# Weight bounds from products of the weight tiles with themselves, and scales kept for four groups of tiles

## The chip, the cores and the metric

The kernel runs on one core of a Trainium2 chip. Its five engines work side by side, each through its own queue in order: TensorE (PE, with its weight loads as PEld), VectorE (DVE), ScalarE (ACT), GpSimd (POOL), and SyncE (SP), which issues the DMAs. The metric is the device time of one execution in microseconds (us); the kernel before takes 956.86 us, the median of 3 runs between 954.78 and 958.99.

## What is computed

Clustered attention is followed by a two-layer network. A query sees only the keys that fall to the same of 16 centroids. The two weight matrices come as 64-bit floats, the other inputs as 32-bit ones; batch 4, 8 heads, 768 positions, head width 64, model width 512, hidden width 2048 (`attn_out` below is `attn` times `v`).

```python
q_assign = np.argmax(np.einsum('bhsd,hcd->bhsc', q_n, c_n), axis=-1)
k_assign = np.argmax(np.einsum('bhsd,hcd->bhsc', k_n, c_n), axis=-1)
mask = q_assign[:, :, :, None] == k_assign[:, :, None, :]
scores = scale * np.matmul(q, k.transpose(0, 1, 3, 2))
scores = np.where(mask, scores, -1000000000.0)
scores = scores - np.max(scores, axis=-1, keepdims=True)
attn = np.exp(scores)
attn = attn / (np.sum(attn, axis=-1, keepdims=True) + 1e-09)
...
x = np.ascontiguousarray(attn_out.transpose(0, 2, 1, 3)).reshape(B * S, H * D)
h = x @ w_in
r = np.maximum(h, 0.0)
g = s * (r * r) + b
return (g @ w_out).astype(np.float32)
```

## The kernel before, in words

Every product is made from float16 pairs, a high and a low part, in three matmuls, so each operand is first scaled by a power of two that a bound on its size gives.

**Units.** The attention is cut into 192 units (one batch, one head, 128 queries). The main loop runs once for each: unit i has its scores on PE (L454, tile `sc`), its maximum on DVE (L463), its exponential on ACT (L473, tile `p`), and one turn later the high part `ph` (L483, `high`), the low part on POOL (L496), and a transposing DMA (L498); the product with the values (L515 to L517, tile `px`) comes five turns later. The first eight units (`RAW`) go through PE transposes instead. `high` casts on POOL for units 8 to 18, then up to unit 36 in turn on DVE (odd) and ACT (even), then on ACT.

**MLP steps.** With a lag of 21 turns (`LAG`), turn i also runs step i-21 of the MLP: 12 matmuls into `h` (L573), three ACT passes (L580 to L583), a POOL subtraction (L588), and two turns later 6 matmuls into `acc` (L600). There are 12 chunks of 16 steps; step ft uses the weight tiles ft of both matrices. `acc`, `h` and `px` have one PSUM buffer each; small helpers use the banks of `h` and `px`.

**Weights.** 32 tiles (16 of each matrix, numbered p, w_in even and w_out odd) go through `weights()`: a load of 512 KB, `rebase` (ACT, L203), `narrow` (two DVE instructions, L207 and L208), and one stage later `bound`: an ACT pass with absolute values (L215 or L217), for w_in also four matmuls with ones (L220) and a DVE reduction (L221). Three stages run ahead of the loop and each turn runs two more, so the last tile is done around turn 15. `finish_w_in` and `finish_w_out` then make one scale for each matrix with a row of tiny DVE instructions into `glob`. `wsplit(ft)` (from turn 17 on, one each turn, ACT L265 and DVE L267) makes the float16 pairs of step ft. At the end of the first chunk `column_sums` (L275, 32 matmuls into `pb`) makes the `bias` row, and two DVE instructions (L608) write out `acc`.

A scheduler orders each engine's queue: code order is the priority, units up to 20 are preferred by 300 instructions (`first_of_all`), and an instruction that isn't ready lets a later one go first.

Of the kernel before, what the change touches and what calls it, by code (L numbers as in the profile page):

```python
# [26 lines left out]
def tile_cluster_attention_mlp(ctx, tc, q, k, v, cent, w_in, w_out, s_in, b_in, out):  # L27
# [183 lines left out]
    def bound(d):  # L211
        w, p, ft = d["w"], d["p"], d["ft"]
        wa = sb.tile([P, KT, P], BF16, tag="wab", name=f"wab_{p}", bufs=2)
        if p % 2:
            A.activation(wa, w, AF.Abs, accum_out=l1[:, ft : ft + 1])  # L215
        else:
            A.activation(wa, w, AF.Abs)  # L217
            pw = ps_h.tile([P, 512], F32, tag="h", name=f"pw_{ft}")
            for t in range(KT):
                nc.tensor.matmul(pw[:, :P], ones, wa[:, t, :], start=(t == 0), stop=(t == KT - 1))  # L220
            V.tensor_reduce(w1[:, ft : ft + 1], pw[:, :P], axis=AX.X, op=ALU.max)  # L221
# [27 lines left out]
    def finish_w_out():
        lc = columns(1, "w")  # L250
        V.tensor_reduce(lc, l1, axis=AX.X, op=ALU.max)
        allmax(glob[:, 4:5], lc, "w")
# [4 lines left out]
        V.tensor_tensor(glob[:, 6:7], sv, glob[:, 4:5], op=ALU.mult)

    def wsplit(ft):
        while narrowed[0] < 2 * NF:  # L260
            next(wgen)
        made = []
        for w, f in ((wi[ft], glob[:, 2:3]), (wo[ft], glob[:, 5:6])):
            e = parts(weight_tile(f"w{'io'[len(made)]}s{ft}"))
            A.activation(e[:, 0], w, AF.Copy, scale=f)  # L265
            yield
            V.scalar_tensor_tensor(e[:, 1], w, f, e[:, 0], op0=ALU.mult, op1=ALU.subtract)  # L267
            made.append(e)
        WSP[ft] = (made[0], made[1].rearrange("p e a f -> p e (a f)"))

    def column_sums():
        pb = ps_m.tile([P, 512], F32, tag="m", name="pb")
        for ft in range(NF):
            for e in range(2):
                nc.tensor.matmul(pb, ones16, WSP[ft][1][:, e, :], start=(ft + e == 0), stop=(ft + e == NF))  # L275
        V.tensor_tensor(glob[:, 7:8], bv, glob[:, 4:5], op=ALU.mult)
        bias.append(weight_tile("bias").rearrange("p a f -> p (a f)"))
        V.tensor_scalar(bias[0], pb, glob[:, 7:8], None, op0=ALU.mult)
# [276 lines left out]
    def mlp_start(b, c):  # L555
        n = f"{b}_{c}"
        xm = XM[(b, c)]
        V.tensor_scalar(xm[:, 5:6], xm[:, 5:6], glob[:, 0:1], None, op0=ALU.mult)
# [5 lines left out]
        V.scalar_tensor_tensor(xm[:, 7:8], xm[:, 6:7], xm[:, 6:7], glob[:, 6:7], op0=ALU.mult, op1=ALU.mult)
# [25 lines left out]

    def mlp_out(b, c, ft):
        n = f"{b}_{c}"
        if ft == 0:
            MS[(b, c)][2] = ps_a.tile([P, CT, DM], F32, tag="acc", name=f"acc_{n}")
        acc = MS[(b, c)][2]
        g = GS.pop((b, c, ft))
        for t in range(CT):
# [1 line left out]
            for gl, wl in ((0, 0), (0, 1), (1, 0)):
                nc.tensor.matmul(acc[:, t, :], g[:, gl, rows], WSP[ft][1][:, wl, :],  # L600
                                 start=(ft == 0 and gl + wl == 0), stop=(ft == NF - 1 and gl == 1))
        if ft == NF - 1:
            _, e, acc = MS.pop((b, c))
            o = sb.tile([P, CT, DM], F32, tag="stage", name=f"o_{n}", bufs=3)
            if b + c == 0:
                column_sums()
            for t in range(CT):
                V.scalar_tensor_tensor(o[:, t, :], acc[:, t, :], e, bias[0], op0=ALU.mult, op1=ALU.add)  # L608
# [150 lines left out]
```

## Time and profile before

| | before |
|---|---|
| median of 3 runs | 956.86 us |
| the profiled execution, its own time | 959.63 us |
| its span, first to last instruction | 957.6 us |
| DMA over the span | 147.36 MB, 154 GB/s |
| HBM read, written | 35.69 MB, 6.29 MB |

The page gives each engine's busy time over the span, then the span in 40 equal slices, each digit a busy share in tenths. A view by windows gives the busy time in chosen stretches of the span, a view by line gives groups of equal instructions with their mean duration, and a view of waits says who waited for whom. The lines are shown where the prediction uses them.

### The profile page before, as it was taken

Reading aid. Unit: us, or ns where it says so; the run is one execution under the profiler, and the core shown is the slowest. Engines: PE = TensorE matmul, PEld = TensorE weight load, DVE = VectorE, ACT = ScalarE, POOL = GpSimd, SP = SyncE. Lnnn points to the kernel's source line nnn. Section 1 sums busy time; section 2 is a strip of 40 time slices with the busy share of each in tenths; the row PEclk is TensorE's granted clock in tenths of the full one; section 3 lists DMA queues with packets and bytes.
Section 4 is the critical chain, followed back from the end, with each engine's and each line's share of the span. In section 5 each row is a group of like instructions: output and inputs, shape, how many; then the busy total and the mean of one; then the engine's idle time right before and its main releaser. Section 6 shows DMA issues by size and latency. Waiting matters only on the chain. (4 is left out here: it accounts for less than half of the span.)

```text
span 957.6 us, 22486 instructions
## 1 busy us (share of the span) xinstructions
PE 831.2 (87%) x8625; PEld 580.0 (61%) x8625; DVE 614.9 (64%) x1400; ACT 709.9 (74%) x1390; POOL 568.9 (59%) x596
## 2 busy tenths in 40 slices
PE   1668446988899999987999999998899999999997
PEld 0456323655567776655676676665666766767664
DVE  8797978888767746566856555487775466463100
ACT  4477656978579888866887988786888888889443
POOL 4012545868468667656676756666776765676321
PEclk9966657999999999999999999999999999999999
DMA  7887974688677777799887757889787866676200
GB/s 187 218 217 217 256 170 94 156 180 152 142 157 165 167 139 163 131 182 197 163 157 152 160 129 162 160 184 207 142 172 154 149 112 150 138 158 138 33 24 22
DMA packets 450299, 147.36 MB, mean 154 GB/s; under 512 B 417936, under 2 KB 446608, under 8 KB 450192
## 3 DMA queue, kind: packets, MB, share of 16 engines
q1 hardware_dynamic: 450192, 145.93, 72.0%
q8 instruction: 67, 1.10, 0.5%
q14 instruction: 40, 0.33, 0.1%
HBM read 35.69 MB, written 6.29 MB: 44 GB/s over the span
## 5 line engine op out<-in xcount | busy, mean ns | idle before, releaser
L496 POOL TENSOR_TENSOR ph<-p,ph 128x768 f16<-128x768 f32 x184 | 314.2, 1707 | 123.7 <-ACT ph L119 82.7
L600 PE MATMUL acc<-wos,g 128*128 128x512 f16 x1152 | 298.5, 381 | 5.0 <-POOL g L588 4.6
L573 PE MATMUL h<-x,wis 128*128 128x256 f16 x2304 | 290.2, 275 | 8.4 <-ACT r L580 4.1
L573 PEld LDWEIGHTS <-wis 128*128 128x128 f16 x2304 | 223.3, 98 | 62.7 <-issue 10.3
L463 DVE TENSOR_REDUCE ssm<-sc 128x1 f32<-128x768 f32 x192 | 181.2, 951 | 30.1 <-PE sc L454 29.5
L588 POOL TENSOR_TENSOR g<-r,g 128x256 f16<-128x256 f32 x192 | 131.9, 688 | 110.0 <-ACT r L583 106.3
L473 ACT ACTIVATE p<-sc,ssm,qsm 128x768 f32<-128x768 f32 x192 | 188.0, 979 | 2.6 <-POOL g L588 0.4
L600 PEld LDWEIGHTS <-g 128*128 128x128 f16 x1152 | 103.8, 98 | 87.9 <-POOL g L588 10.3
L580 ACT ACTIVATE r<-h,cf 128x256 f32<-128x256 f32 x192 | 89.4, 466 | 77.0 <-PE h L573 62.1
L119 ACT ACTIVATE ph<-p 128x768 f16<-128x768 f32 x164 | 136.3, 831 | 9.1 <-DMA PT<-ph 8.7
L515 PE MATMUL px<-vh,PT 128*128 128x65 f16 x1104 | 119.6, 196 | 10.8 <-DVE xs L527 4.6
L470 ACT ACTIVATE ssm<-ssm,lift,qsm 128x1 f32<-128x1 f32 x192 | 73.2, 381 | 74.5 <-DVE ssm L463 73.4
L516 PE MATMUL px<-vl,PT 128*128 128x64 f16 x1104 | 119.6, 193 | 0.0
L517 PE MATMUL px<-vh,PT 128*128 128x65 f16 x1104 | 119.6, 194 | 0.0
L454 PE MATMUL sc<-KA,QA 128*128 128x384 f16 x384 | 99.8, 342 | 20.4 <-ACT p L473 17.4
L515 PEld LDWEIGHTS <-PT 128*128 128x128 f16 x1104 | 103.6, 98 | 18.5 <-issue 8.9
L516 PEld LDWEIGHTS <-PT 128*128 128x128 f16 x1104 | 103.2, 100 | 13.7 <-issue 5.3
L454 PE MATMUL sc<-KB,QB 128*128 128x384 f16 x384 | 100.4, 344 | 8.7 <-DMA QB<-qb 8.7
L517 PEld LDWEIGHTS <-PT 128*128 128x128 f16 x1104 | 103.5, 98 | 3.4
L582 ACT ACTIVATE g<-r 128x256 f16<-128x256 f32 x192 | 79.3, 413 | 3.6
L583 ACT ACTIVATE r<-r 128x256 f32<-128x256 f32 x192 | 78.8, 410 | 3.1
L523 DVE TENSOR_SCALAR ssm<-px 128x2 f32<-128x2 f32 x92 | 14.3, 155 | 79.9 <-PE px L517 79.8
(156 smaller groups left out, 1039.9 us busy)
## 6 DMA issues: line engine op xcount, KB each, us to landing
wst<-in_moe_w_in_dram SPq DMA_DIRECT2D x16, 512.0 KB, 4.9
wst<-in_moe_w_out_dram SPq DMA_DIRECT2D x16, 512.0 KB, 4.6
kn<-in_k_dram SPq DMA_DIRECT2D x16, 384.0 KB, 3.9
qn<-in_q_dram SPq DMA_DIRECT2D x24, 256.0 KB, 3.6
vn<-in_v_dram SPq DMA_DIRECT2D x16, 384.0 KB, 5.0
out_dram<-o SPq DMA_DIRECT2D x12, 512.0 KB, 3.7
PT<-ph SPq DMA_TRANSPOSE x184, 3.4
x<-xn SPq DMA_TRANSPOSE x48, 2.5
```

The costliest lines, as they stand in the source:

```text
L119: A.activation(dst, src, AF.Copy)
L454: last_score[0] = nc.tensor.matmul(sc[:, e, :HALF], X[:, col, :], y[:, h * S + e * HALF : h * S + (e + 1) * HALF], start=st, stop=not st)
L463: last_max[0] = V.tensor_reduce(SM[i // 4][:, 0, j : j + 1], U[i]["sc"], axis=AX.XY, op=ALU.max, negate=True)
L473: last_exp[0] = A.activation(p.rearrange("p (a b) -> p a b", a=2), u["sc"], AF.Exp, bias=bi, scale=u["scale"], **total)
L496: G.tensor_tensor(u["ph"][:, 1, :], u["p"], u["ph"][:, 0, :], op=ALU.subtract)
L515: nc.tensor.matmul(o1, PT[:, kt, :], vh[:, h, kt, : D + 1], start=(kt == 0), stop=False)
L516: nc.tensor.matmul(o, PT[:, kt, :], vl[:, h, kt, :], start=False, stop=False)
L517: nc.tensor.matmul(o1, PT[:, T + kt, :], vh[:, h, kt, : D + 1], start=False, stop=(kt == T - 1))
L573: nc.tensor.matmul(ph[:, :CW], WSP[ft][0][:, wl, kt, :], XS[(b, c, kt)][:, :, xl, :], start=(i == 0), stop=(i == len(terms) - 1))
L580: A.activation(r, ph[:, :CW], AF.Relu, scale=MS[(b, c)][0])
L588: G.tensor_tensor(g[:, 1, :], r, g[:, 0, :], op=ALU.subtract)
L600: nc.tensor.matmul(acc[:, t, :], g[:, gl, rows], WSP[ft][1][:, wl, :], start=(ft == 0 and gl + wl == 0), stop=(ft == NF - 1 and gl == 1))
```

## The change

- `bound` no longer makes absolute values on ACT. It takes the upper halves of a tile's floats as bfloat16 and multiplies each 128x128 block with itself (four matmuls for a tile, w_out too), into one PSUM bank for four tiles; one DVE reduction takes the maximum, which bounds the squared norms of the columns. It runs for every fourth tile.
- `finish_group` replaces the two finishers. It runs four times, after 8 tiles each, and makes from the maxima both scales of that group of four steps (through halved exponents in place of square roots). The last one also makes a scale for all groups, `uni`.
- `wsplit(ft)` waits only for the tiles of its group, and the loop runs one stage of `weights()` each turn, not two.
- In the first chunk `acc` is taken out after every four steps with the group's own factor and added up in `first_o`; `mlp_start` runs four times there. Later chunks put the groups' differences into the factor of L580 (`cf`, now four columns), and go on as before.
- `column_sums` works in four pieces through `pb`.
- `high` casts on POOL up to unit 30.
- `ones` goes, `ident` and `ones16` move into buffers of other tiles.

```diff
+    def floor4(dst, src):
+        V.tensor_scalar(dst, src, 2.0 ** -60, 2.0 ** 60, op0=ALU.max, op1=ALU.min)
+        V.tensor_scalar(dst.bitcast(I32), dst.bitcast(I32), 0x7F000000, None, op0=ALU.bitwise_and)
...
-        if p % 2:
-            A.activation(wa, w, AF.Abs, accum_out=l1[:, ft : ft + 1])
-        else:
-            A.activation(wa, w, AF.Abs)
-            pw = ps_h.tile([P, 512], F32, tag="h", name=f"pw_{ft}")
+    def bound(pairs):
+        pw = ps_h.tile([P, 512], F32, tag="h", name=f"pw_{pairs[0][0]['ft']}")
+        for j, d in enumerate(sum(pairs, [])):
+            wa = d["w"].bitcast(BF16).rearrange("p a (f z) -> p a f z", z=2)[:, :, :, 1]
             for t in range(KT):
-                nc.tensor.matmul(pw[:, :P], ones, wa[:, t, :], start=(t == 0), stop=(t == KT - 1))
-            V.tensor_reduce(w1[:, ft : ft + 1], pw[:, :P], axis=AX.X, op=ALU.max)
+                nc.tensor.matmul(pw[:, j * P : (j + 1) * P], wa[:, t, :], wa[:, t, :], start=(t == 0), stop=(t == KT - 1))
+        ft = pairs[0][0]["ft"]
+        V.tensor_reduce(wsq[:, ft : ft + 2, :], pw.rearrange("p (f e q) -> p f e q", e=2, q=P), axis=AX.X, op=ALU.max)
+        if (ft + 2) % GROUP == 0:
+            finish_group(ft // GROUP)
...
+            p = i - 3
+            if p >= 0 and p % 4 == 3:
+                bound([[live[p - 3], live[p - 2]], [live[p - 1], live[p]]])
...
+    def finish_group(k):
+        g = [gl[:, e, k : k + 1] for e in range(10)]
+        lc = columns(2, f"w{k}")
+        V.tensor_reduce(lc, wsq[:, k * GROUP : (k + 1) * GROUP, :].rearrange("p f e -> p e f"), axis=AX.X, op=ALU.max)
+        allmax(gsq, lc, f"w{k}")
+        V.tensor_scalar(g[0], gsq[:, 0:1], DM * 1.04, None, op0=ALU.mult)
+        V.tensor_scalar(g[4], gsq[:, 1:2], 1.04, None, op0=ALU.mult)
+        for e in (0, 4):
+            bits = g[e].bitcast(I32)
+            V.tensor_scalar(bits, bits, 1, None, op0=ALU.logical_shift_right)
+            V.tensor_scalar(bits, bits, 127 << 22, None, op0=ALU.add)
+        floor2(V, g[1], g[0])
...
+        V.tensor_tensor(g[6], sv, g[4], op=ALU.mult)
+        V.tensor_tensor(g[7], bv, g[4], op=ALU.mult)
+        V.tensor_tensor(g[8], g[0], g[3], op=ALU.mult)
+        V.tensor_tensor(g[9], g[1], g[3], op=ALU.mult)
...
     def wsplit(ft):
-        while narrowed[0] < 2 * NF:
-            next(wgen)
+        k = ft // GROUP
+        while narrowed[0] < 2 * GROUP * (k + 1):
+            next(wgen, None)
...
-        copy(G if i < LAG - 2 else V if i < LAG + NF and i % 2 else A, u["ph"][:, 0, :], u["p"])
+        copy(G if i < LAG + 10 else V if i < LAG + NF and i % 2 else A, u["ph"][:, 0, :], u["p"])
...
+        if first:
+            o = first_o
+            if ft == NF - 1:
                 column_sums()
             for t in range(CT):
+                if k == 0:
+                    V.tensor_scalar(o[:, t, :], acc[:, t, :], e, None, op0=ALU.mult)
+                else:
+                    V.scalar_tensor_tensor(o[:, t, :], acc[:, t, :], e, o[:, t, :], op0=ALU.mult, op1=ALU.add)
+                if ft == NF - 1:
+                    V.tensor_tensor(o[:, t, :], o[:, t, :], bias[0], op=ALU.add)
...
-        some(wgen, 2)
+        some(wgen, 1)
```

The first place is DVE's queue behind the maximum of unit 10 (counted from 0), in the stretch in which the weights come in; `wi` and `wo` are weight tiles, `wst` their loads, `qsm` the scales of the next queries. Before:

```order
L463 TENSOR_REDUCE ssm_864<-sc_975 128x1
L207 TENSOR_SCALAR wi_740<-wi_740 128x512
L68 TENSOR_SCALAR qsm_1_0_829<-qsm_1_0_829 128x2
L221 TENSOR_REDUCE w_128<-pw_774 128x1
L208 SCALAR_TENSOR_TENSOR wi_740<-wst_741,wi_740 128x512
L69 TENSOR_SCALAR qsm_1_0_829<-qsm_1_0_829 128x2
L207 TENSOR_SCALAR wo_783<-wo_783 128x512
L70 TENSOR_SCALAR qsm_1_0_829<-qsm_1_0_829 128x2
L208 SCALAR_TENSOR_TENSOR wo_783<-wst_784,wo_783 128x512
```

The same place now, with the first `finish_group` (`gl` are its ten columns):

```order
L483 TENSOR_REDUCE ssm_798<-sc_877 128x1
L253 TENSOR_SCALAR gl<-gl 128x1 x2
L102 TENSOR_REDUCE qsm_1_0_733<-am_q_1_0_816 128x2
L60 TENSOR_SCALAR gl<-gl 128x1
L64 TENSOR_SCALAR gl<-gl 128x1
L221 TENSOR_REDUCE wsq<-pw_942 128x4
L72 TENSOR_SCALAR qsm_1_0_733<-qsm_1_0_733 128x2
L61 TENSOR_SCALAR gl<-gl 128x1
L65 TENSOR_SCALAR gl<-gl 128x1
```

Behind this unit no weight tile is narrowed any more, where six and a part of a seventh were before; tiny instructions on single columns stand there in their place.

The second place is DVE's queue behind the maximum of unit 25, where the MLP runs beside the units. Before (`wos` is a float16 pair of `wsplit`):

```order
L463 TENSOR_REDUCE ssm_1820<-sc_1860 128x1
L98 TENSOR_REDUCE qsm_2_0_1795<-am_q_2_0_1847 128x2
L68 TENSOR_SCALAR qsm_2_0_1795<-qsm_2_0_1795 128x2
L69 TENSOR_SCALAR qsm_2_0_1795<-qsm_2_0_1795 128x2
L267 SCALAR_TENSOR_TENSOR wos_1952<-wo_783,glob,wos_1952 128x512
L70 TENSOR_SCALAR qsm_2_0_1795<-qsm_2_0_1795 128x2
```

The same place now:

```order
L483 TENSOR_REDUCE ssm_1797<-sc_1843 128x1
L246 TENSOR_REDUCE amb_w_1750<-wsq 128x2
L210 TENSOR_SCALAR wo_1636<-wo_1636 128x512
L211 SCALAR_TENSOR_TENSOR wo_1636<-wst_1637,wo_1636 128x512
L282 SCALAR_TENSOR_TENSOR wos_1942<-wo_1013,gl,wos_1942 128x512
L102 TENSOR_REDUCE gsq<-am_w_1752 128x2
L248 TENSOR_SCALAR gl<-gsq 128x1
L249 TENSOR_SCALAR gl<-gsq 128x1
L252 TENSOR_SCALAR gl<-gl 128x1 x2
L253 TENSOR_SCALAR gl<-gl 128x1 x2
L60 TENSOR_SCALAR gl<-gl 128x1
L587 TENSOR_SCALAR xm_737<-xm_737,gl 128x1
```

Narrowing (now L210 and L211) and the third `finish_group` now stand between the maxima of units whose MLP steps run. One unit further the first group of `acc` is taken out:

```order
L643 TENSOR_SCALAR first_o<-acc_0_0_1644,es_0_1505 128x512 x2
L282 SCALAR_TENSOR_TENSOR wos_2001<-wo_1102,gl,wos_2001 128x512
L211 SCALAR_TENSOR_TENSOR wi_1781<-wst_1782,wi_1781 128x512
L547 TENSOR_TENSOR xs_1928<-px_1889,ssm_1443 128x128
L282 SCALAR_TENSOR_TENSOR wis_2003<-wi_1214,gl,wis_2003 128x512
L483 TENSOR_REDUCE ssm_1797<-sc_2011 128x1
```

Nothing like the first row stood there before; the maximum of unit 27, the last row, comes behind it.

More of the change, by code (lines that the diff above doesn't have):

```diff
@@ L169, in weight_tile @@
         return cp.tile([P, KT, P], F32, tag="w", name=name, bufs=2 * NF + 1)
-    w1 = const([P, NF], F32, "w1")
-    l1 = const([P, NF], F32, "l1")
-    glob = const([P, 12], F32, "glob")
+    GROUP = 4
+    NG = NF // GROUP
+    wsq = const([P, NF, 2], F32, "wsq")
+    gsq = const([P, 2], F32, "gsq")
+    gl = const([P, 10, NG], F32, "gl")
+    uni = const([P, 2], F32, "uni")
     bias = []
@@ L271, in column_sums @@
     def column_sums():
[L272 to L278, printed above, removed]
+        ones16 = sb.tile([P, P], F16, tag=f"oe{2 * T}", name="ones16", bufs=1)
+        G.memset(ones16, 1.0)
+        for k in range(NG):
+            pb = ps_m.tile([P, 512], F32, tag="m", name=f"pb{k}")
+            n = 2 * GROUP
+            for j in range(n):
+                nc.tensor.matmul(pb, ones16, WSP[k * GROUP + j // 2][1][:, j % 2, :], start=(j == 0), stop=(j == n - 1))
+            if k == 0:
+                bias.append(weight_tile("bias").rearrange("p a f -> p (a f)"))
+                V.tensor_scalar(bias[0], pb, gl[:, 7, k : k + 1], None, op0=ALU.mult)
+            else:
+                V.scalar_tensor_tensor(bias[0], pb, gl[:, 7, k : k + 1], bias[0], op0=ALU.mult, op1=ALU.add)
     def onehot(pa, nb, name, dst, mul, add, eng):
@@ L589, in mlp_gl @@
         GS[(b, c, ft)] = g
+    first_o = const([P, CT, DM], F32, "first_o")
     def mlp_out(b, c, ft):
         n = f"{b}_{c}"
-        if ft == 0:
-            MS[(b, c)][2] = ps_a.tile([P, CT, DM], F32, tag="acc", name=f"acc_{n}")
+        first = b + c == 0
+        span = GROUP if first else NF
+        k = ft // GROUP
+        if ft % span == 0:
+            MS[(b, c)][2] = ps_a.tile([P, CT, DM], F32, tag="acc", name=f"acc_{n}_{ft}")
         acc = MS[(b, c)][2]
@@ L598, in mlp_out @@
             rows = slice(t * P, t * P + P)
[L599 to L605, printed above, removed]
+            for gi, wl in ((0, 0), (0, 1), (1, 0)):
+                nc.tensor.matmul(acc[:, t, :], g[:, gi, rows], WSP[ft][1][:, wl, :],
+                                 start=(ft % span == 0 and gi + wl == 0), stop=(ft % span == span - 1 and gi == 1))
+        if ft % span < span - 1:
+            return
+        e = MS[(b, c)][1][:, k : k + 1] if first else MS[(b, c)][1][:, 0:1]
+        if first:
+            o = first_o
+            if ft == NF - 1:
                 column_sums()
             for t in range(CT):
+                if k == 0:
+                    V.tensor_scalar(o[:, t, :], acc[:, t, :], e, None, op0=ALU.mult)
+                else:
+                    V.scalar_tensor_tensor(o[:, t, :], acc[:, t, :], e, o[:, t, :], op0=ALU.mult, op1=ALU.add)
+                if ft == NF - 1:
+                    V.tensor_tensor(o[:, t, :], o[:, t, :], bias[0], op=ALU.add)
+        else:
+            o = sb.tile([P, CT, DM], F32, tag="stage", name=f"o_{n}", bufs=3)
+            for t in range(CT):
                 V.scalar_tensor_tensor(o[:, t, :], acc[:, t, :], e, bias[0], op0=ALU.mult, op1=ALU.add)
+        if ft == NF - 1:
+            MS.pop((b, c))
             nc.sync.dma_start(out[b * S : (b + 1) * S].rearrange("(p t) e -> p t e", t=T)[:, c * CT : (c + 1) * CT, :], o)
@@ L715, in tile_cluster_attention_mlp @@
         if 0 <= m < NS:
-            if steps[m][2] == 0:
-                mlp_start(*steps[m][:2])
+            if steps[m][2] % GROUP == 0:
+                mlp_start(*steps[m][:2], steps[m][2] // GROUP)
             mlp_in(*steps[m])
```

70 lines of the change are left out of this document (32 added, 38 removed).

## The prediction

> **What bounds the kernel now.** First the page's first row and its 40 slices (24 us each):
>
> ```profile
> PE 831.2 (87%) x8625; PEld 580.0 (61%) x8625; DVE 614.9 (64%) x1400; ACT 709.9 (74%) x1390; POOL 568.9 (59%) x596
> ...
> PE   1668446988899999987999999998899999999997
> ...
> DVE  8797978888767746566856555487775466463100
> ...
> PEclk9966657999999999999999999999999999999999
> ```
>
> From about the twelfth slice PE is full and DVE is not; before it DVE is the fuller one and PE's clock is low. The change touches only the weights and the first chunk, so the early part decides. I cut it at the maxima (L463) of units 0, 21, 45 and 57. The view by windows of this line alone (busy us and count; the last window holds unit 57's start too):
>
> ```profile
> 34.60:150.40 115.80, 19.86 (x21) 0.67 0.83 211
> 150.40:274.50 124.10, 22.64 (x24) 0.94 0.73 152
> 274.50:322.00 47.50, 11.43 (x13) 1.00 0.82 172
> ```
>
> The view by windows; columns are length, then busy us of PE, PEld, DVE, ACT, POOL, each with its count, then clock, DMA share and GB/s. The last two rows show how full DVE gets over long and short times:
>
> ```profile
> 34.60:150.40 115.80, 71.72 (x528) 52.93 (x526) 96.97 (x204) 76.06 (x150) 39.85 (x36) 0.67 0.83 211
> 150.40:274.50 124.10, 106.14 (x1074) 70.35 (x1075) 99.96 (x212) 91.22 (x177) 78.84 (x71) 0.94 0.73 152
> 274.50:322.00 47.50, 47.03 (x562) 33.49 (x559) 34.27 (x75) 41.80 (x80) 36.78 (x38) 1.00 0.82 172
> 36.00:162.00 126.00, 76.99 (x609) 57.22 (x610) 106.01 (x227) 83.31 (x162) 44.70 (x40) 0.66 0.79 201
> 48.00:72.00 24.00, 15.86 (x116) 12.74 (x117) 22.97 (x53) 18.49 (x37) 3.70 (x5) 0.68 0.82 217
> ```
>
> Stretch 1 (21 units, 115.8 us) has DVE 83.7% busy (96.97 / 115.8) and PE 62%. Stretch 2 (24 units) has PE at 86% and DVE at 81%. Stretch 3 is PE alone (47.03 of 47.5). DVE can hold 84% for 126 us (106.01 / 126) and 95.7% for 24 us (22.97 / 24). The waits of stretch 1 say the same: ACT waits for DVE's maxima.
>
> ```profile
> ACT ssm L470 <- DVE ssm L463: 16.3, 11, 6.0
> ...
> PE pw L220 <- ACT wab L217: 7.5, 3, 4.5
> ```
>
> **The change, part by part: narrowing moves.** Groups by line in stretch 1 (count, then busy us and mean ns):
>
> ```profile
> L208 DVE SCALAR_TENSOR_TENSOR wi<-wst,wi 128x512 uint32<-128x512 uint32 x14 | 15.5, 1106 | 0.1
> L208 DVE SCALAR_TENSOR_TENSOR wo<-wst,wo 128x512 uint32<-128x512 uint32 x15 | 12.8, 851 | 0.1
> L207 DVE TENSOR_SCALAR wi<-wi 128x512 int32<-128x512 int32 x14 | 8.1, 577 | 4.4 <-ACT wi L203 4.4
> L207 DVE TENSOR_SCALAR wo<-wo 128x512 int32<-128x512 int32 x15 | 6.8, 453 | 3.7 <-ACT wo L203 3.7
> ...
> L221 DVE TENSOR_REDUCE w<-pw 128x1 f32<-128x128 f32 x15 | 4.2, 281 | 1.4 <-PE pw L220 1.4
> ```
>
> Before, 29 of the 32 tiles are narrowed in stretch 1 and none in stretch 2. In the new order 18 stand in stretch 1 and 11 (5 `wi`, 6 `wo`) in stretch 2. A `wi` costs 1.106 + 0.577 = 1.68 us, a `wo` 0.851 + 0.453 = 1.30: **16.2 us of DVE leave stretch 1 and enter stretch 2**.
>
> **The bounds.** The 16 reductions of 0.281 go, 15 of them in stretch 1 (-4.2). Eight reductions over 512 columns come, five in stretch 1, three in stretch 2. The old finishers go from stretch 1; four `finish_group` come, two in each stretch. Rows for single instructions (min / median / max ns):
>
> ```profile
> L60 DVE TENSOR_SCALAR glob<-glob x2: 155/155/155, 132.3 to 135.6; 128x1 f32<-128x1 f32 x2
> ...
> L257 DVE TENSOR_TENSOR glob<-sv,glob x1: 481/481/481, 136.5 to 136.5; 128x1 f32<-128x1 f32 x1
> L276 DVE TENSOR_TENSOR glob<-bv,glob x1: 148/148/148, 136.9 to 136.9; 128x1 f32<-128x1 f32 x1
> ```
>
> ```profile
> L101 DVE TENSOR_REDUCE amb_q<-qn 128x2 bf16<-128x512 f32 x3 | 2.1, 686 | 5.7 <-DMA qn<-in_q_dram 5.7
> L98 DVE TENSOR_REDUCE qsm<-am_q 128x2 f32<-128x256 f32 x24 | 10.0, 418 | 11.6 <-PE am_q L97 11.6
> ```
>
> A reduction over 512 costs some 0.686: +3.4 and +2.1. One `finish_group` is 21 tiny instructions at 0.155 (3.3), four products of two columns, which lie between 0.148 and 0.481 (I take the middle, 1.3 for the four), and a reduction over 256 (0.418): 4.9 us, so +9.8 in each stretch (8.7 to 11.2 by the two ends). The old finishers were 13 tiny ones, the two products and a reduction of 0.28: 2.9.
>
> **The first chunk.** Writing out `acc` four times makes eight instructions and two additions of `bias` in place of two (L608); `pb` is read four times in place of one (L278); three more `mlp_start`, each three small ones at 0.155 and four on `glob` columns (two shown).
>
> ```profile
> L608 DVE SCALAR_TENSOR_TENSOR o<-acc,xm,bias 128x512 f32<-128x512 f32 x24 | 16.9, 744 | 47.4 <-PE acc L600 46.7
> ...
> L278 DVE TENSOR_SCALAR bias<-pb,glob 128x512 f32<-128x512 f32 x1 | 0.7, 742 | 0.0
> ```
>
> ```profile
> L558 DVE TENSOR_SCALAR xm<-xm,glob x12: 200/213/215, 156.0 to 903.7; 128x1 f32<-128x1 f32 x12
> ...
> L564 DVE SCALAR_TENSOR_TENSOR xm<-xm,glob x12: 211/232/674, 159.2 to 904.9; 128x1 f32<-128x1 f32 x12
> ```
>
> 8 x 0.744 = 6.0, 3 x 0.742 = 2.2, 3 x 1.3 = 4.0: +12.2 in stretch 2.
>
> **The casts.** Units 19 to 30 cast on POOL: six leave DVE, six ACT.
>
> ```profile
> L121 DVE CAST ph<-p 128x768 f16<-128x768 f32 x9 | 5.8, 644 | 0.3 <-ACT p L473 0.2
> ...
> L121 POOL CAST ph<-p 128x768 f16<-128x768 f32 x11 | 11.6, 1054 | 19.0 <-ACT p L473 16.9 <-issue 2.1
> ```
>
> -3.9 us of DVE in stretch 2. One `wsplit` moves ahead into stretch 1 by the order, 0.8 us:
>
> ```profile
> L267 DVE SCALAR_TENSOR_TENSOR wos<-wo,glob,wos 128x512 f16<-128x512 f32 x14 | 11.5, 818 | 0.8 <-ACT wos L265 0.8
> ```
>
> POOL gets 12 x 1.054 = 12.6 us on its 78.8; 91 us in 124 or more still fit.
>
> **Sum of DVE.** Stretch 1: 97.0 - 16.2 - 4.2 - 2.9 + 3.4 + 9.8 + 0.8 = 87.7. Stretch 2: 100.0 + 16.2 + 2.1 + 9.8 + 12.2 - 3.9 = **136.4, more than the 124.1 us that the stretch lasts**. So DVE takes the place of PE as what holds stretch 2, and hides what else is added there. At 83.7% as now, stretch 1 becomes 104.8 us (-11.0). For stretch 2 I take 90%, the middle of the two shares above: 136.4 / 0.90 = 151.6 (+27.5). Its floor, DVE never idle, is +12.3; at 84% it is +38.
>
> **What lies beside it.** ACT loses the absolute values:
>
> ```profile
> L215 ACT ACTIVATE wab<-wo 128x512 bf16<-128x512 f32 x15 | 9.3, 623 | 2.6 <-DVE wo L208 2.5
> L217 ACT ACTIVATE wab<-wi 128x512 bf16<-128x512 f32 x14 | 8.7, 623 | 5.5 <-DVE wi L208 4.3 <-DVE ssm L523 1.1
> ```
>
> 18 us of 76 in stretch 1, where ACT isn't the bound: nothing, or at best the 7.5 us for which PE waited behind them. PE gets 128 products for 64:
>
> ```profile
> L220 PE MATMUL pw<-wab,ones 128*128 128x128 bf16 x60 | 8.9, 295 | 10.8 <-ACT wab L217 7.5 <-DVE w L221 2.5 <-DVE oe_k L287 0.8
> ```
>
> 0.148 us each (8.9 / 60): +3 us in stretch 1, where PE idles 44 us, and 48 of them, +7.1, in stretch 2; read in every second half-word, which no row shows, between that and twice. PE's 106 + 7 to 14 stay under 136. If DVE were not the bound, 7 to 14 us would show. The 11 loads that move with their tiles (5.8 MB) cost SP nothing new: the same number, behind the same transposes; at 211 GB/s for 0.83 of the DMA engines they are 23 us of these, and stretch 2 has a quarter free (0.73).
>
> The new waits: scores and values behind an `acc` matmul on PE wait until DVE has taken the group before out (three more times, 1.5 us each and its place in the queue); `h` waits for the reduction of `pw` in its bank; step 12 waits for the last `finish_group`. Behind all of them stands DVE itself, whose time is counted; alone each would be 0 to 3 us, some 15 together, which I keep for the upper end.
>
> **What comes back later.** In the new PE order 26 steps of the MLP precede the scores of unit 45, 24 before; at unit 55 both are level. Pieces from the chain of waits:
>
> ```profile
> 724.55 1.31 PE h L573 x12
> 726.53 1.29 PE acc L600 x6
> ```
>
> Two steps are 5.2 us of PE work that stretch 3 no longer has; as it is PE's own, I take 4 back (0 to 5.2). From unit 57 on the queues hold the same work.
>
> **Sum:** -11.0 + 27.5 - 4 = +12.5 on the span of 957.6. The profiled execution took 959.63, 2 us around its span, so 972.1 for such a one; it lay 2.8 over the median 956.86, which gives **969.4 us**.
>
> **A rule against the casts.** The narrowing instruction with two inputs from SBUF varies threefold, a reduction of PSUM doesn't:
>
> ```profile
> L208 DVE SCALAR_TENSOR_TENSOR wi<-wst,wi x16: 675/692/2153, 26.1 to 127.1; 128x512 uint32<-128x512 uint32 x16
> ...
> L463 DVE TENSOR_REDUCE ssm<-sc x192: 935/950/960, 34.6 to 881.8; 128x1 f32<-128x768 f32 x192
> ```
>
> The Trainium skill, SBUF — State Buffer, section "Who interferes with whom", says that a VectorE instruction with two SBUF inputs and a GpSimd instruction that reads SBUF lock each other out for a whole instruction, whichever starts first, and that a reduction never does. By that rule the trace agrees, and narrowing beside a fuller POOL would cost more, as the third rival prices it.
>
> **Rivals.** (1) *Faster*: the early waits, not DVE's work, hold stretch 1 (PE behind ACT's absolute values, ACT behind late maxima), and both stretches run at the 95.7%: 91.6 (-24.2), 142.5 (+18.4), -5.2: -11, **946 us**. For it: the 7.5 us of waits go. Against: over 126 us DVE never kept more than 84%. It decides if unit 21 comes by 18 us or more earlier. (2) *No change*: stretch 1 as forecast, stretch 2 at 95.7%: -11 + 18.4 - 5.2 = +2, **959 us**. (3) *Much slower*: POOL and DVE hold each other up. POOL was busy 34% of stretch 1 (39.85) and 64% of stretch 2 (78.84), so the 0.4 us by which L208 on `wi` lies over its median doubles on 11 tiles: +4.6 us, 141 in all, and at the long-time share of 84.1% 167.7 us (+43.6): with -11 and -4 +29, **985 us**.
>
> **How the numbers follow.** Forecast 0.52, (1) 0.18, (2) 0.15, (3) 0.15. The forecast's own range is 957 to 980 (stretch 2 at 98% to 85%). For 8 in 10 the range takes in most of (1) and (3) and the 15 us of waits: 947 to 988. About 0.5% is what a measurement of this kernel can tell from no change, 952.1 to 961.6: same gets (2) and the forecast's lower fringe, 0.20; faster (1) without its fringe, 0.17; slower the rest, 0.63.
>
> **What would show it.** The maximum of unit 21 near 139 us, that of unit 45 near 291; between them DVE at 136 us and some 90%, PE under 80%. Wrong if unit 45 comes before 275, if DVE has under 125 us there, or if the end moves without these marks. Later stretches should be as long as before.

## The result and the profile after

The changed kernel takes **990.82 us** (median of 4, 990.04 to 992.09); the kernel before took 957.92 beside it (954.78 to 961.27). The ratio is 1.0344, 95% interval 1.0305 to 1.0383: slower by 33 us where the forecast had 12.5. The profiled span is 988.2 against 957.6, so the traces hold 30.6 us of it.

The page's first row and slices of the changed kernel (one slice is 24.7 us):

```profile
PE 851.0 (86%) x8696; PEld 590.7 (60%) x8696; DVE 633.6 (64%) x1500; ACT 688.9 (70%) x1336; POOL 576.5 (58%) x607
...
PE   0578558767899899899789999998999999999997
...
DVE  6687699979767756557776646567966656464100
...
PEclk9975557979999899999999999998999999999999
```

Among the first twelve slices DVE now has nines in 6, 7, 8 and 10, where it had them in 3 and 5; PE, at eight or nine tenths from the eighth slice on before (but for one slice), is so only from the eleventh. Next the windows cut at the maxima (now L483) of units 0, 21, 45 and 57, and then stretch 2 cut once more, at unit 39. Columns are as in the prediction: length, busy us of PE, PEld, DVE, ACT, POOL, clock, DMA share, GB/s.

```profile
36.30:145.20 108.90, 74.49 (x551) 55.61 (x549) 83.36 (x206) 54.47 (x99) 40.10 (x37) 0.64 0.81 178
145.20:302.70 157.50, 124.94 (x1206) 82.26 (x1207) 133.59 (x317) 97.09 (x188) 87.14 (x87) 0.89 0.72 150
302.70:350.10 47.40, 43.16 (x491) 30.26 (x490) 30.94 (x71) 37.30 (x70) 36.59 (x37) 0.93 0.98 179
...
145.20:253.80 108.60, 80.67 (x766) 52.78 (x767) 100.48 (x243) 67.61 (x129) 61.36 (x58) 0.84 0.75 159
253.80:302.70 48.90, 44.27 (x442) 29.48 (x440) 33.11 (x76) 29.48 (x60) 25.77 (x30) 1.00 0.65 130
```

The same last cut in the kernel before:

```profile
150.40:231.60 81.20, 67.98 (x721) 46.13 (x721) 72.39 (x150) 66.21 (x130) 56.69 (x47) 0.95 0.74 156
231.60:274.50 42.90, 38.16 (x353) 24.22 (x354) 27.57 (x63) 25.00 (x48) 22.15 (x25) 0.92 0.71 145
```

| term of the span, us | forecast | measured |
|---|---|---|
| up to unit 0 | 0 | +1.7 (36.3 for 34.6) |
| stretch 1, units 0 to 21 | -11.0 | -6.9 (108.9 for 115.8) |
| stretch 2, units 21 to 45 | +27.5 | +33.4 (157.5 for 124.1) |
| stretch 3, units 45 to 57 | -4 | -0.1 (47.4 for 47.5) |
| behind unit 57 | 0 | +2.5 (30.6 less the rest) |

So the signs are those of the forecast, and each size is off to the same side: the 18.1 us by which the span misses the forecast are the 1.7, 4.1, 5.9, 3.9 and 2.5 of the five rows. The finer cut shows where stretch 2 grew: units 21 to 39 by 27.4 us (108.6 for 81.2), with DVE busy 92.5% (100.48 of 108.6; before 89%), and units 39 to 45 by 6.0, with PE busy 91% and DVE 68%. By these shares stretch 2 has two parts with different limits, one behind the other.

In stretch 1 of the changed kernel, the view of waits (what waited for what: us, times, longest) has ACT standing twice as long for late maxima as the 16.3 us of before, though DVE's work there fell from 96.97 to 83.36 us:

```profile
ACT ssm L490 <- DVE ssm L483: 32.4, 12, 9.3
```

and a window inside it, in the changed kernel and in the kernel before, suggests what held the units in place of DVE:

```profile
85.00:105.00 20.00, 16.65 (x119) 13.57 (x119) 10.39 (x21) 7.02 (x15) 9.27 (x10) 0.50 0.77 169
```

```profile
85.00:105.00 20.00, 12.93 (x81) 10.49 (x79) 15.83 (x30) 14.68 (x31) 8.05 (x7) 0.59 0.99 247
```

DVE is half idle there (10.39 of 20 us) and PE, granted half its clock (0.50), is 83% busy. That PE held the units there is read from this window alone.

### The profile page after: what moved, and what is told of

It reads as the page before. It is cut to its first block, busy times and chain, and to the rows that moved or that the text cites. A ratio compares the mean times of both kernels' runs of the same rounds, so it can differ in the third digit from the quotient of the medians.

```text
span 988.2 us, 22639 instructions
## 1 busy us (share of the span) xinstructions
PE 851.0 (86%) x8696; PEld 590.7 (60%) x8696; DVE 633.6 (64%) x1500; ACT 688.9 (70%) x1336; POOL 576.5 (58%) x607
## 4 chain that ended last, share of the span: by engine, by line
PE 47%; DVE 19%; DMA 11%; issue 6%; ACT 5%; POOL 5%; SPq 2%; POOLq 0%; DVEq 0%; ACTq 0%
PE h L600 16%; PE acc L632 15%; PE sc L474 6%; DVE ssm L483 4%; DMA PT<-ph 3%; POOL ph L516 2%; DMA qn<-in_q_dram 2%; PE px L535 2%; PE px L537 2%; PE px L536 2%; DMA QA<-qa 2%; PE px L530 2%; ACT p L493 1%; DMA QB<-qb 1%; POOL g L615 1%
## 5 line engine op out<-in xcount | busy, mean ns | idle before, releaser
L600 PE MATMUL h<-x,wis 128*128 128x256 f16 x2304 | 294.5, 277 | 14.7 <-DMA x<-xn 6.4
L600 PEld LDWEIGHTS <-wis 128*128 128x128 f16 x2304 | 225.8, 99 | 73.2 <-issue 19.0
L483 DVE TENSOR_REDUCE ssm<-sc 128x1 f32<-128x768 f32 x192 | 181.3, 951 | 32.5 <-PE sc L474 32.2
L632 PEld LDWEIGHTS <-g 128*128 128x128 f16 x1152 | 104.7, 99 | 89.6 <-POOL g L615 7.6
L607 ACT ACTIVATE r<-h,cf 128x256 f32<-128x256 f32 x192 | 89.5, 466 | 81.8 <-PE h L600 71.6
L119 ACT ACTIVATE ph<-p 128x768 f16<-128x768 f32 x158 | 131.3, 831 | 17.7 <-DMA PT<-ph 17.7
L535 PE MATMUL px<-vh,PT 128*128 128x65 f16 x1104 | 123.6, 199 | 14.0 <-DVE xs L547 9.1
L536 PE MATMUL px<-vl,PT 128*128 128x64 f16 x1104 | 123.2, 196 | 0.0
L537 PE MATMUL px<-vh,PT 128*128 128x65 f16 x1104 | 123.0, 197 | 0.0
L474 PE MATMUL sc<-KA,QA 128*128 128x384 f16 x384 | 103.1, 351 | 21.9 <-ACT p L493 19.0
L535 PEld LDWEIGHTS <-PT 128*128 128x128 f16 x1104 | 105.7, 100 | 21.6 <-issue 13.6
L536 PEld LDWEIGHTS <-PT 128*128 128x128 f16 x1104 | 105.5, 101 | 13.0 <-issue 6.1
L474 PE MATMUL sc<-KB,QB 128*128 128x384 f16 x384 | 102.5, 351 | 10.2 <-DMA QB<-qb 10.2
L537 PEld LDWEIGHTS <-PT 128*128 128x128 f16 x1104 | 105.7, 100 | 3.4
```

The source lines that it names most:

```text
L119: A.activation(dst, src, AF.Copy)
L474: last_score[0] = nc.tensor.matmul(sc[:, e, :HALF], X[:, col, :], y[:, h * S + e * HALF : h * S + (e + 1) * HALF], start=st, stop=not st)
L483: last_max[0] = V.tensor_reduce(SM[i // 4][:, 0, j : j + 1], U[i]["sc"], axis=AX.XY, op=ALU.max, negate=True)
L535: nc.tensor.matmul(o1, PT[:, kt, :], vh[:, h, kt, : D + 1], start=(kt == 0), stop=False)
L536: nc.tensor.matmul(o, PT[:, kt, :], vl[:, h, kt, :], start=False, stop=False)
L537: nc.tensor.matmul(o1, PT[:, T + kt, :], vh[:, h, kt, : D + 1], start=False, stop=(kt == T - 1))
```

## The experiments

Sixteen kernels ran, each timed against the kernel before on the same chip. The table gives the ratio with its interval, then three marks of the profiled execution: the starts of the maxima of units 21 and 39, and the span. Unless "before" is named, a kernel is the changed one with the edits shown.

| run | ratio (95%) | unit 21 | unit 39 | span |
|---|---|---|---|---|
| before | 1 | 150.4 | 231.6 | 957.6 |
| the change | 1.0344 (1.0305-1.0383) | 145.2 | 253.8 | 988.2 |
| pw_bank_m | 1.0316 (1.0263-1.0369) | 139.8 | 248.4 | 982.3 |
| two_per_turn | 1.0496 (1.0456-1.0535) | 162.2 | 268.7 | 1008.6 |
| casts_back | 1.0259 (1.0205-1.0313) | 143.6 | 257.1 | 988.3 |
| few_finish | 1.0337 (1.0298-1.0376) | 140.0 | 250.7 | 993.3 |
| one_group | 1.0134 (1.0102-1.0166) | 151.1 | 240.6 | 972.1 |
| two_casts | 1.0287 (1.0251-1.0324) | 160.6 | 246.2 | 985.1 |
| acc_once | 1.0295 (1.0257-1.0333) | 145.9 | 255.7 | 989.5 |
| two_casts_acc | 1.0256 (1.0198-1.0314) | 161.3 | 247.0 | 985.6 |
| after_act | 1.0178 (1.0150-1.0205) | 141.6 | 246.3 | 974.9 |
| before_casts (before) | 1.0180 (1.0141-1.0219) | 151.0 | 255.7 | 972.4 |
| casts_act (before) | 1.0012 (0.9990-1.0035) | 151.3 | 236.7 | 960.7 |
| extra_mid (before) | 1.0150 (1.0111-1.0189) | 161.3 | 245.4 | 968.3 |
| extra_pb (before) | 1.0146 (1.0113-1.0178) | 163.9 | 249.3 | 979.0 |
| pin_mid (before) | 1.0116 (1.0072-1.0160) | 152.0 | 246.9 | 971.0 |
| pin_pb (before) | 1.0076 (1.0050-1.0103) | 150.0 | 231.0 | 963.0 |
| pin_late (before) | 1.0104 (1.0068-1.0140) | 150.1 | 231.2 | 965.8 |

**The bank of `h`.** The changed kernel's waits between 180 and 220 us show the MLP's matmuls into `h` held by a reduction of the bounds in their bank:

```profile
PE h L600 <- DVE wsq L221: 3.8, 2, 2.8
```

pw_bank_m takes the bank of `px`:

```diff
-        pw = ps_h.tile([P, 512], F32, tag="h", name=f"pw_{pairs[0][0]['ft']}")
+        pw = ps_m.tile([P, 512], F32, tag="m", name=f"pw_{pairs[0][0]['ft']}")
```

> The changed kernel with one edit: the products of the weight tiles with themselves (pw) use the PSUM bank of px in place of that of h. Theory DVE (stretch 2 lasts as long as DVE's work at a share of 85%): DVE's work is the same, so 988 to 993 us. Theory BANK (the MLP stands still while pw holds the bank of h, 183.5 to 192.4 and 199.1 to 215.3 us in the trace of the changed kernel, and DVE idles there): 8 to 14 us less, 977 to 983, with stretch 2 (maxima of units 21 to 45) at 144 to 150 us where it took 157.5, and DVE's share there over 89%.

It measured 1.0316, which the intervals do not part from the change's 1.0344. Units 21 to 39 took 108.6 us, as in the change; what the span shows (982.3 for 988.2) lies in stretch 1, where unit 21 came 5.4 us earlier. The bank is not what made stretch 2 long.

**Narrowing early again**, and **the casts where they were**:

```diff
-        some(wgen, 1)
+        some(wgen, 2)      # two_per_turn
-        copy(G if i < LAG + 10 else V if i < LAG + NF and i % 2 else A, u["ph"][:, 0, :], u["p"])
+        copy(G if i < LAG - 2 else V if i < LAG + NF and i % 2 else A, u["ph"][:, 0, :], u["p"])   # casts_back
```

> The changed kernel with two stages of the weights each turn, as before. By the rows DVE's work in stretch 1 (units 0 to 21) goes from 83 to about 109 us and in stretch 2 from 134 to about 106. Theory DVE: stretch 1 at 84% is 130 (+21), stretch 2 falls to PE's 126 to 130 (-28 to -31): 980 to 985 us. Theory BANK: pw is then mostly done before the MLP starts, so another 8 to 10 less: 970 to 976. If neither holds and the spreading itself was a gain: over 991.

> The changed kernel with the casts of units 19 to 30 on DVE and ACT in turn, as before. Theory DVE: six casts of 0.55 to 0.65 us more for DVE in stretch 2 at 85%: +4 to +5, 994 to 996 us. Theory PORT (casts on POOL hold up DVE's two-input instructions, wis at 1.12 us where it took 0.86): the instructions shorten by 3 to 6 us in sum, 984 to 990 us. Theory BANK: within 3 us of 990.8.

two_per_turn is the slowest of all, over 991, as if the spreading itself were a gain (two_casts, below, speaks against that): unit 21 comes at 162.2, and units 21 to 39 still take 106.5 us, with DVE busy only 84 of them. casts_back has more of DVE's work (106.56 us between units 21 and 39 for 100.48) and is not slower than the change (1.0259 against 1.0344, intervals that just touch), against the DVE theory. Its 987.63 us lies in the PORT theory's range, but not for that reason: the splits of `wi` (L282) fell from 1122 to 855 ns, and those of `wo` rose from 911 to 1295. So the casts on POOL cost something of their own. **before_casts** puts only them into the kernel before:

> The kernel before with the casts of units 19 to 30 on POOL: that part of the change alone. Theory DVE: 4 us of DVE and 5 of ACT less in stretch 2, which PE holds there: 0 to -4, 953 to 959 us. Theory POOL (a fuller POOL delays the low parts, and with them the transposes and loads in SP's queue): 5 to 12 us more, 963 to 970 us.

```diff
-        copy(G if i < LAG - 2 else V if i < LAG + NF and i % 2 else A, u["ph"][:, 0, :], u["p"])
+        copy(G if i < LAG + 10 else V if i < LAG + NF and i % 2 else A, u["ph"][:, 0, :], u["p"])
```

It lost 1.8%, more than either theory allowed. Its windows from unit 21 to unit 39:

```profile
151.00:255.70 104.70, 77.51 (x765) 51.86 (x766) 78.73 (x159) 67.60 (x126) 69.05 (x63) 0.84 0.62 132
```

No engine is above 76% there, and the stretch is 23.5 us longer than before. Among what waits is SP's queue, from which the transposes of `ph` (L498) go out; its waits in before_casts from unit 21 to 30 (151 to 208.6 us), and those of the kernel before from unit 21 to 30 (150.4 to 187.8):

```profile
SPq L498 <- POOL g L588: 20.1, 5, 6.0
SPq L390 <- POOL qb L292: 7.3, 2, 4.0
SPq L498 <- POOL ph L121: 6.7, 1, 6.7
SPq L498 <- POOL ph L496: 4.3, 2, 3.6
```

```profile
SPq L498 <- POOL g L588: 9.6, 5, 3.3
SPq L498 <- POOL qb L292: 6.2, 1, 6.2
SPq L498 <- POOL ph L496: 3.4, 2, 2.2
SPq L498 <- POOL qa L373: 3.4, 1, 3.4
```

Transposes waited for POOL 31.1 us (20.1 + 6.7 + 4.3) where they had waited 22.6 (9.6 + 6.2 + 3.4 + 3.4), and the other transposes of this queue stand behind them. A cast and the subtraction of `low` for one unit stand on POOL one after the other, with the MLP's `g` between them. So POOL had room by its busy time, and its order may have had none. But the window of before_casts is also 54% longer (57.6 us for 37.4), so the waits for POOL take no larger share of it. That the casts on POOL cost the time is shown; that they cost it through this chain is not.

**What the parts cost by themselves.** Narrowing early, casts as before, once with one group (one_group, the new bounds alone) and once with four (two_casts):

```diff
-    GROUP = 4
+    GROUP = NF               # one_group only
-        some(wgen, 1)
+        some(wgen, 2)        # both, and the casts as in casts_back
```

> The changed kernel with GROUP = 16 (all tiles one group, one finish, the first chunk taken out once), two stages of the weights each turn and the casts as before: the new bounds alone. Theory DVE: DVE's work is that of before within 1 us in stretch 1 and 4 us in stretch 2, ACT has 21 us less: 952 to 962 us. Theory PRODUCTS (the 128 products and their bank are the harm, in whatever stretch): 968 us or more.

> The changed kernel with two stages of the weights each turn and the casts as before; four groups stay. Two stages alone gave 1010 us, where POOL was in the chain of waits of stretch 2. Theory TWO BOUNDS (DVE where the tiles are narrowed, POOL where it also casts): stretch 1 as in that run, 127 us, stretch 2 back to 126 to 134 where that run took 154: 980 to 990 us. Theory FIRST CHUNK (taking acc out in groups holds PE and the MLP whatever else runs): stretch 2 stays at 150 or more, 1003 to 1012 us.

The new bounds alone cost 1.3% and the four groups 1.5% more. one_group lies over the DVE theory's range and in that of PRODUCTS, but by no mechanism that the runs show: stretch 1 is as long as before although ACT's absolute values are gone (114.2 us for 115.8), no products stand behind it, and the loss comes between units 33 and 42. From unit 21 to 39 DVE worked 74.70 of 89.5 us, less than the 89% of before, so its work doesn't explain the 8.3 us; what does was not found. two_casts, at 987.15 us, is in the range of TWO BOUNDS and far under that of FIRST CHUNK: with the casts off POOL, units 21 to 39 took 85.6 us where two_per_turn had 106.5.

Three runs look for the four groups' cost. few_finish copies the ten columns of group 0 for the other groups, acc_once takes the first chunk's sum out once and `pb` in one piece, two_casts_acc is two_casts with that edit too:

```diff
+        if k:                                     # few_finish
+            V.tensor_copy(gl[:, :, k], gl[:, :, 0])
...
+            return
-        span = GROUP if first else NF             # acc_once
-        k = ft // GROUP
+        span = NF
+        k = 0
```

> The changed kernel, where groups 1 to 3 take over the ten columns of group 0 with one copy: their own maxima across partitions and scales are left out (the reductions of pw stay). Theory DVE: three times some 4.4 us of DVE go, 8 to 9 of them in stretch 2: at 85% 9 to 12 us less, 979 to 982 us. Theory BANK: the finish of a group isn't what holds h: 0 to 4 us less, 987 to 991.

> The changed kernel, where the first chunk's acc is taken out once and pb is summed in one piece, as before; the groups' own factors are left out of both. Theory DVE: 7 to 8 us of DVE less in stretch 2, at 85% 8 to 10 us: 981 to 984 us. Theory FIRST CHUNK: stretch 2, which took 157.5 us, falls by 18 us or more: 973 us or less.

> The changed kernel with two weight stages per turn and the casts as before (the run of that kind gave 987 where the kernel before had 960), and the first chunk's sum taken out once with pb in one piece (the groups' own factors are left out). It is the run with one group (973) and three more finish_group, which stand in stretch 1 or at its end. FIRST CHUNK theory (the four sums make the 14 us between the two runs): 973 to 978. FINISH theory (the finishes make them): 983 to 988. DVE theory counts both, by their work over 0.92: 975 to 981.

few_finish won 5.2 us at unit 21 and 3.1 at unit 39 and lost them again by unit 45; its windows from 39 to 45:

```profile
250.70:306.40 55.70, 47.25 (x446) 30.97 (x445) 34.57 (x77) 29.00 (x56) 23.34 (x27) 0.91 0.58 110
```

55.7 us for the change's 48.9, with DVE busy 62%. The expectation of a gain at the end failed. acc_once gained nothing that the intervals show, against both its theories. Both runs took 4 us of DVE's work away between units 21 and 39 (96.19 and 96.44 for 100.48), and the stretch got no shorter (110.7 and 109.8 us for 108.6). two_casts_acc, at 984.87 us, landed where the finish theory put it: three more finishes than one_group, and 1.2% more time. Their work is in stretch 1, whose DVE work is larger by 11.3 us there (106.88 against 95.61, in 125.6 against 114.2 us): the instructions of the finishes, and five splits of the weights (L282) that may now start earlier.

**Casts on ACT**, off DVE and from unit 19 on off POOL, in the kernel before (casts_act) and in the change (after_act); both end with this line:

```diff
+        copy(G if i < LAG - 2 else A, u["ph"][:, 0, :], u["p"])
```

> The kernel before, with the nine casts (0.644 us each) that DVE makes for odd units 19 to 35 given to ACT (0.83 us each). DVE theory: 5.8 us less of DVE before unit 39, which comes 4 to 6 us earlier, and so does the end: 954 to 957 where the kernel before has 960. ACT theory (ACT, 82% busy there, becomes late with the exponentials): 0 to 7 us slower.

> The changed kernel with all casts of units 19 to 36 on ACT: none of them on POOL, as in the run with the casts as before, and none on DVE. The run with the casts as before gave 987.6 where the kernel before had 961. DVE theory: 9 x 0.644 us less than there, so 979 to 983. ACT theory: 988 to 995. POOL theory (what the casts cost on POOL is all that matters): 986 to 989.

In the kernel before it made no difference that can be told. DVE's work from unit 21 to 39 didn't even fall (72.56 us for 72.39: later work moved up into the room), and ACT's rose from 66.21 to 74.14. In the change, 977.85 us is a little better than the DVE theory's 979 to 983 and rules out the ACT and POOL theories; of the versions that keep the four groups it is the best, 1.0178. Units 21 to 39 took 104.7 us with 93.8 of DVE, against 113.5 with 106.6 in casts_back.

**Idle DVE work.** 44 narrowing instructions on a spare tile in the kernel before, in turns 22 to 32 or 40 to 50:

```diff
+        if 22 <= i < 33:        # extra_mid; extra_pb: 40 <= i < 51
+            extra()
```

> The kernel before, and in each of turns 22 to 32 two pairs of idle narrowing instructions (256 columns, on a spare tile) on DVE: 44 instructions, estimated at half the rows of L207 and L208, 13 to 18 us in all, before unit 39. Nothing else changes: no wait, no POOL, no PE. DVE theory (the time until unit 39 is done is the work of DVE divided by some 0.92, and whatever comes later there stays to the end): units 21 to 39 take 95 to 101 us in place of 81, first MLP step of the second chunk 14 to 20 us later, end 12 to 20 us later, 972 to 980. QUEUE theory (DVE's fullness only goes along with it; POOL's, SP's and PE's queues set the pace): DVE fills its idle time first (81.2 less 72.4 is 9), end 0 to 7 us later.

> The kernel before, with the same 44 idle instructions in turns 40 to 50, behind unit 39. There DVE is busy 64% (27.6 of 42.9 us) and PE 89%. DVE theory, with the end of unit 39 and of unit 55 as the two gates: the work fits beside PE, end 0 to 5 us later. If every us of DVE work counts wherever it stands: 13 to 18 us later, as in the run with turns 22 to 32.

Both lost 15 us, and not for the reason under test: nothing tied the instructions to a turn, so the scheduler that sets each engine's order put them at the start, between 3 and 47 us in the traces, and unit 0 was late by 6.3 and 7.5 us. From unit 21 on extra_mid has the kernel before's stretch (84.1 for 81.2). They tell nothing of stretch 2, so they were run again with each piece tied behind the maximum of its turn:

```diff
+            with behind(last_max[0]):
+                extra()         # pin_mid 22-32, pin_pb 40-50, pin_late 64-74
```

> The same 44 idle DVE instructions (16.2 us measured) as before, now each tied behind the maximum (L463) of its turn, turns 22 to 32, so that they stand on DVE between units 21 and 33. In the two runs before they had no such tie, and the program had put them at its very start. DVE theory (units 21 to 39 last as long as DVE's work there divided by 0.92): 81.2 us become 94 to 99, the end 12 to 18 us later than it would be without them. QUEUE theory: 81 to 90 us. What the edit does at the start (some 6 us there in the two runs before) is read from unit 21 and taken off.

> The same, tied to turns 40 to 50, where DVE is 64% busy and PE 89%. DVE theory: units 39 to 57 (90.4 us before) last at most 5 us longer. If each us of DVE counts wherever it stands: 12 to 16 us longer.

> The same, tied to turns 64 to 74, where PE is full: units 57 to 96 (175.8 us before) last 0 to 3 us longer by the DVE theory, 12 to 16 us if each us of DVE counts. Beside the two others this run shows what the edit itself costs at the start.

The windows of pin_mid, from unit 21 to unit 39:

```profile
152.00:246.90 94.90, 74.11 (x721) 48.90 (x721) 92.93 (x194) 68.42 (x130) 54.29 (x47) 0.88 0.62 133
```

20.5 us more of DVE's work (92.93 less 72.39) made the stretch 13.7 us longer, in the DVE theory's range, and filled DVE to 98%; the other 6.8 us went into its idle time. This doesn't part the theories: the queue theory's 81 to 90 us reckoned with 16.2 us of added work, and a stretch with 92.93 us of it can't be shorter than that. It shows that DVE can be filled to 98% and then sets the pace, not what its work costs while it still idles. At the end the span is 13.4 us longer, and the ratio 1.0116 says 11. In pin_pb, units 39 to 57 took 99.6 us, 9.2 more, between the two theories, with 16.8 us more of DVE's work; 5.4 of them were left in the span. pin_late lost 2.6 us from unit 57 to 96, as the DVE theory said, but 8.2 at the end, most of it between units 96 and 112, far behind the edit. By their windows added DVE work is cheaper where PE is fuller, not free; by the whole time the three places can't be told apart (1.0116, 1.0076 and 1.0104, with overlapping intervals), for a reason that these runs don't show.

**Units 21 to 39 in the other versions.** The windows of two_per_turn, few_finish and acc_once, all with the casts on POOL, then of two_casts and after_act, with the casts off it:

```profile
162.20:268.70 106.50, 79.10 (x764) 52.29 (x765) 84.15 (x184) 65.45 (x123) 66.57 (x63) 0.79 0.66 127
140.00:250.70 110.70, 81.37 (x755) 53.71 (x756) 96.19 (x191) 68.40 (x130) 64.29 (x60) 0.85 0.76 159
145.90:255.70 109.80, 81.12 (x788) 53.23 (x789) 96.44 (x243) 69.03 (x131) 65.39 (x61) 0.86 0.79 162
...
160.60:246.20 85.60, 68.81 (x709) 46.26 (x710) 79.36 (x168) 66.08 (x126) 53.51 (x47) 0.95 0.77 143
141.60:246.30 104.70, 77.80 (x803) 52.16 (x804) 93.82 (x255) 78.13 (x147) 56.34 (x49) 0.90 0.82 174
```

In all six kernels that cast units 19 to 30 on POOL the stretch took 104.7 to 110.7 us, whether DVE had 78.7 us of work in it (before_casts) or 100.5 (the change). Where the casts are off POOL it goes with DVE's work, from 81.2 us with 72.4 (before) to 113.5 with 106.6 (casts_back), though not closely (94.9 us in pin_mid, 104.7 in after_act, with 93 to 94). So the change has two limits of nearly the same size here, DVE's work and the casts on POOL, and lowering one alone brought little.

## Why the prediction came out right in direction and short in size

- **What holds stretch 2: right in part.** "DVE takes the place of PE as what holds stretch 2" fits up to unit 39: there DVE's work rose by 28.1 us and the time by 27.4. Its 100.48 us alone are more than the 81.2 us of before, so 19.3 us would be lost with nothing else changed. But the casts on POOL alone made this stretch nearly as long (104.7 us in before_casts), so DVE's work isn't shown to be what sets it. The mark for DVE's work, 136 us, was met at 133.59, in part by luck, as terms were off to opposite sides (below); those for the maxima were not (145.2 us for 139 at unit 21, 302.7 for 291 at unit 45).
- **The failed step: one share of DVE for the whole stretch, with PE's added work hidden behind it.** 136.4 / 0.90 took DVE's idle time in stretch 2 to fall to 15.2 us. It stayed at 23.9, where it had been 24.1: the share came out at 84.8%, and the time grew by DVE's added work in full (33.4 us for 33.6). Most of that idle time, 15.8 us, lies from unit 39 to 45 (before 15.3), where PE was 91% busy. There PE had 6.1 us more work (44.27 for 38.16), and the time grew by 6.0. The forecast had the cause in hand: the MLP runs two steps ahead at unit 45 (26 for 24 in front of its scores), 5.2 us of PE's work. Of these it took 4 off stretch 3 and put none into stretch 2: "PE's 106 + 7 to 14 stay under 136" counts the products alone and takes PE's work as hidden. The 48 products took only 4.1 us of PE; its busy time rose by 18.8 in all, with more MLP matmuls and, up to unit 39, a lower granted clock (0.84 for 0.95). That PE sets the pace behind unit 39 is read from the shares: DVE's work rose there too (33.11 for 27.57), and in few_finish PE was only 85% busy in the same units.
- **Stretch 1: -6.9 for -11.0.** DVE's work fell further than forecast (83.36 for 87.7). The share fell too, to 76.5%, for which the 83.7% "as now" had no reason once DVE was relieved; the window above suggests PE at half clock and late maxima. But the size of this miss is hardly to be told: six versions with 82.8 to 86.0 us of DVE's work in stretch 1 took 103.0 to 110.3 us there, one profiled execution each, and the forecast's 104.8 lies among them.
- **Finishing a group was mis-sized, 4.9 us for about 2.8** (11.2 us of DVE's time for the four, each instruction counted only until the next one starts). In the change's timeline (start, duration) such instructions start 0.06 to 0.07 us apart and are recorded with 0.14:

```profile
83.15 0.14 DVE L256 TENSOR_SCALAR gl<-gl 128x1 f32<-128x1 f32 x1
83.21 0.14 DVE L257 TENSOR_SCALAR gl<-gl 128x1 f32<-128x1 f32 x1
83.27 0.14 DVE L261 TENSOR_SCALAR gl<-gl 128x1 int32<-128x1 int32 x1
83.33 0.14 DVE L263 TENSOR_SCALAR gl<-gl 128x1 f32<-128x1 f32 x1
```

  The sum added the recorded durations, so it counted each tiny instruction about twice. The Trainium skill, Perfetto Trace Analysis, section "Optimizing Scalar/DVE Operations", says that an instruction's profiled latency is about twice the time for which it keeps the engine; these rows agree.
- **Narrowing was under-sized.** Eleven `wi` and `wo` tiles, 22 instructions, were put at 16.2 us; the 23 instructions of these rows of the change, from unit 21 to 39, took 18.6:

```profile
L211 DVE SCALAR_TENSOR_TENSOR wi<-wst,wi 128x512 uint32<-128x512 uint32 x6 | 5.8, 974 | 0.1
L211 DVE SCALAR_TENSOR_TENSOR wo<-wst,wo 128x512 uint32<-128x512 uint32 x6 | 4.6, 773 | 0.2
L210 DVE TENSOR_SCALAR wo<-wo 128x512 int32<-128x512 int32 x6 | 4.4, 726 | 1.9 <-ACT wo L206 1.9
L210 DVE TENSOR_SCALAR wi<-wi 128x512 int32<-128x512 int32 x5 | 3.8, 767 | 0.5 <-ACT wi L206 0.5
```

- **"I take 4 back" failed.** This is the other side of the failed step: the MLP was two steps ahead at unit 45 and PE's work in stretch 3 fell by 3.9 us (43.16 for 47.03), but its length didn't (47.4 for 47.5): DMA was at 0.98 where it had been 0.82. The first step of the MLP's second chunk ends in the change, as before, close behind the maximum of unit 39 (258.5 us, before 234.8), and that of the third close to unit 55's (339.9, before 311.1), so a lead inside a chunk is waited away; in before_casts, 44 us passed between the end of the first chunk's last step and that of the next. That DMA took PE's place is read from the share and was not tried.
- **"91 us in 124 or more still fit" failed as a reason.** This term was put at nothing, and the casts on POOL cost 1.8% in before_casts and 2.1% between two_casts and two_per_turn, with POOL busy only 66 and 63% between units 21 and 39. In the change itself they cost less: casts_back is 0.8% faster, with touching intervals, as DVE's work rises there. The third rival named POOL and DVE as holding each other up, and its 985 us lies nearest to the result, but not by its mechanism: narrowing as a whole was only 2.4 us longer than forecast, and its two-input rows (974 and 773 ns) lie under those of before (1106 and 851).
- **The new waits** were right as small: the bank of `h` and the four sums gave nothing that can be told from zero. That ACT lost its absolute values brought nothing that can be told, as forecast (stretch 1 of one_group).

Open: by what chain the casts on POOL hold the units up, the 8.3 us of one_group between units 21 and 39, and the up to 5 us that several runs gain or lose behind unit 96 with the same work. No version beat the kernel before.

## What to carry to other kernels

A stretch may have two bounds one behind the other: cut it where the fuller engine changes, count each engine's added work at full price in the part that it bounds, and put work that moves ahead into the part where it now stands. Room on an in-order queue is not its idle share: ask for the moved instruction what stands behind it and who waits for that. A share of busy time from before holds only as long as the same engine is what is waited for, and work that is meant as a probe must be tied to its place, and its place read from the trace, before its time means anything. A probe that fills its engine shows a limit, not the price of the work below that limit.

## What the runs showed of the hardware

The same single-input instruction of DVE on 256 columns took 301 ns in the program's first 48 us (extra_mid), where POOL was busy 9.7 of 48 us, and 547 ns in turns 22 to 32 (pin_mid), where POOL was busy 57%:

```profile
L231 DVE TENSOR_SCALAR spare<-spare 128x256 int32<-128x256 int32 x22 | 6.6, 301 | 0.1
```

```profile
L231 DVE TENSOR_SCALAR spare<-spare 128x256 int32<-128x256 int32 x22 | 12.0, 547 | 0.0
```

The prediction spoke of the lock between DVE and POOL for instructions with two inputs only. The Trainium skill, SBUF — State Buffer, section "Who interferes with whom", names `tensor_scalar` in the modes that use both ports among those that can take the shared pair, and these rows fit that; no run changed POOL alone. So of the 23.5 us that the 44 idle instructions took in pin_mid, 7.3 us (23.5 less the 16.2 of extra_mid) came from their surroundings.
